# How the last four blocks of an output projection join its sum in a decode attention kernel

## The chip, the core and the metric

The kernel runs on one core of one Trainium2 chip. TensorE (PE) multiplies, VectorE (DVE) and ScalarE (ACT) work on vectors, GpSimd (POOL) only fills constants here, and SyncE (SP) issues transfers. The metric is the device time of one execution in microseconds (us); for several runs the median is given.

## The reference

One decode step for two sequences (batch 2, one token, width 512). A layer norm of `x` feeds two branches. The first is attention of 32 query heads on 8 key/value heads, over the last 4096 positions of a cache, and a projection by `wo` (4096 x 512). The second is a small gated network, whose result gates the first:

```python
x = A_x
xn = _layernorm(x, axis=-1)
s = _A_ref(xn, A_k_cache, A_v_cache, A_wq, A_wo)     # softmax(q k / sqrt(128)) v, then @ wo
g = _silu(_B_ref(xn, B_w_in, B_w_sp, B_b_sp, B_w_out))
return x + s * g
```

All is f32. Keys and values of the window are 64 MB of the 89.4 MB that the kernel reads; `wo` is 8 MB.

## The kernel before, in words

Every large transfer is issued by SP into a ring of four slots of 4 MB: `w_in`, `w_out`, two halves of `wq`, then keys and values in turn for eight units (a unit is two key/value heads of one sequence), then `wo`. The gated branch and the queries are computed first. For each unit, DVE transposes the keys (`turn`), PE multiplies them in shares (`shares`, `add_shares`), DVE and ACT make the softmax, and PE multiplies the values (`values`, `scale_out`, `collect`). The transposed outputs of all heads end in `oT`, 32 columns for each of 32 blocks, of which two columns hold the two sequences.

`wo` comes in 32 blocks of 128 rows by 512 columns (256 KB). They arrive in seven transfers (line 423): 8 and 8 blocks in one slot, 8 in a second, and 4, 2, 1, 1 in a third. So blocks 24 to 27 come together, then 28 and 29, then 30, then 31, each transfer with a semaphore of its own that PE waits for ahead of the first matmul that reads it.

The tail (lines 480 to 500) adds `oT` times the blocks in two ways.

- *By shares*: block n is one matmul of 512 columns into rows 32g to 32g+31 of the PSUM bank `part`, with g = n mod 4. So each of the four groups of 32 rows holds the sum of a fourth of the blocks, over all 512 columns. ACT copies the bank to `parts` in SBUF, and `spread_quarters` (line 250) adds the four shares: for each quarter of the columns, one matmul with the constant `rowm` sums the four groups into rows 32g to 32g+31 of a second bank `so`.
- *By column quarters*: block n is four matmuls of 128 columns, each straight into its quarter of `so`. That is four instructions in place of one, and no copy stands between them and the result.

Before the change, blocks 0 to 29 go by shares (`EARLY = 30`). Then come the copy, the spread, which opens the accumulation in `so`, and blocks 30 and 31 by quarters, which close it. DVE multiplies `so` by the gate, adds `x`, and SP and ACT each store one sequence.

The order on each engine is the order of the program text (`InOrder` keeps it), so on PE an instruction that waits holds up all that follow. Since that helper records every operation, all rows of the profile have its line, L37; they are told apart by the names of their tiles.

Of the kernel before, what the change touches and what calls it, by code (L numbers as in the profile page):

```python
# [42 lines left out]
def kernel(  # L43
# [23 lines left out]
    DC = D // G  # L67
# [13 lines left out]
    def slot(name):  # L81
        return ring.tile([P, SLOT], F32, tag="slot", name=name)

    def const(name, *shape):
        return cst.tile([P, *shape], F32, tag=name, name=name)

    def bank(name, tag):
        return ps.tile([P, 512], F32, tag=tag, name=name, bufs=BANKS[tag])
# [12 lines left out]
    for a in range(2):  # L101
        t = slot(f"wq{a}")
# [37 lines left out]
    oT = const("oT", 32, 32)  # L140
# [61 lines left out]
    for k in range(KT):  # L202
        for g in range(G):
            pe.matmul(
                pz[32 * g : 32 * g + 32, :], xnT[:, k, :], ap(win[:, k, :], g * FQ, [[FH, 2], [1, FQ]]),
                start=(k == 0), stop=(k == KT - 1),
# [43 lines left out]
    def spread_quarters(dst, shares, start=True, stop=True):  # L250
        for g in range(G):
            pe.matmul(
                dst[32 * g : 32 * g + 32, :], rowm, shares[:, g * DC : (g + 1) * DC], start=start, stop=stop,
            )

    yp = bank("y", "sh")
    for j in range(FT):
        g = j % G
# [14 lines left out]
    for k in range(KT):  # L273
        for r in range(2):
            for g in range(G):
# [3 lines left out]
                    start=(k == 0), stop=(k == KT - 1),  # L279
# [145 lines left out]
    for i, piece in enumerate(pieces):  # L425
        t = slot(f"wo{i}").rearrange("p (j d) -> p j d", d=D)
# [50 lines left out]
    gather(last)  # L477


    EARLY = 30  # L480
    part = bank("part", "sh")
    for n in range(EARLY):
        t, a = blocks[n]
        g = n % G
        pe.matmul(part[32 * g : 32 * g + 32, :], oT[:, n, :], t[:, a, :], start=(n < G), stop=(n >= EARLY - G))
    parts = sb.tile([P, D], F32, tag="shs", name="parts")
    act.activation(parts, part, AF.Copy)
    so = bank("so", "mo")[:, :DC]
    spread_quarters(so, parts, stop=False)
    for n in range(EARLY, 32):  # L490
        t, a = blocks[n]
        for g in range(G):
            pe.matmul(
                so[32 * g : 32 * g + 32, :], oT[:, n, :], t[:, a, g * DC : (g + 1) * DC], start=False, stop=(n == 31),
            )
    res = const("res", DC)
    dve.tensor_mul(res, so, gate)
# [31 lines left out]
```

## Time and profile before

| what | value |
|---|---|
| median of 3 runs | 219.26 us (218.83 to 219.28) |
| profiled execution | 219.14 us |
| its span, first to last instruction | 217.4 us |
| mean granted TensorE clock | 0.851 |
| PE busy | 156.1 us (72%) |
| DVE busy | 108.6 us (50%) |
| ACT busy | 44.0 us (20%) |
| read from HBM | 89.40 MB, 411 GB/s over the span |

Times in the profile count from the start of the span. A row of the timeline has the start, the length, the engine, the operation, the tiles (out<-in), the shape and the count of a group of equal instructions; in brackets stands how long the engine was idle before and what ended that. PEld rows are weight loads of TensorE, PE rows its matmuls. The chain of waits goes back from the last instruction through whatever released each step.

### The profile page before, as it was taken

What the parts mean: (1) busy time and instruction counts of PE and PEld (TensorE: products, weight loads), DVE (VectorE), ACT (ScalarE), POOL (GpSimd) and SP (SyncE); (2) the same over time, 40 slices, a digit from 0 to 9 for tenths busy, and PEclk for the clock granted to TensorE, in tenths of its full rate; (3) what the DMA queues carried; (4) which work ended last, traced back from release to release, by engine and by line L of the source; (5) the groups of instructions that cost most, each with busy time, mean ns of one, the idle gap of its engine ahead of it and who ended that gap; (6) DMA issues with size and microseconds to landing.
All of it is one profiled execution on the core that took longest, in us unless ns stands there. A gap on an engine that the chain in (4) does not pass through costs nothing.

```text
span 217.4 us, 2207 instructions
## 1 busy us (share of the span) xinstructions
PE 156.1 (72%) x854; PEld 43.4 (20%) x854; DVE 108.6 (50%) x176; ACT 44.0 (20%) x109; POOL 2.6 (1%) x14
## 2 busy tenths in 40 slices
PE   0173185519959948975996797469959949997991
PEld 0121121101212212211221221322221212232211
DVE  3505411579787089148707932594577189221001
ACT  5003310002221421122114212120430421142001
POOL 4000000000000000000000000000000000000000
PEclk9997579955988995998599799757996996999599
DMA  7999999999999999999999999999999999999970
GB/s 254 430 444 446 416 442 419 446 416 452 416 452 410 443 422 446 416 452 416 436 425 428 434 428 419 446 416 452 410 440 425 440 422 440 410 425 423 416 296 4
DMA packets 3937, 89.54 MB, mean 412 GB/s; under 512 B 454, under 2 KB 470, under 8 KB 856
## 3 DMA queue, kind: packets, MB, share of 16 engines
q1 hardware_dynamic: 3912, 89.40, 96.2%
q8 instruction: 7, 0.11, 0.2%
q10 hardware_dynamic: 16, 0.01, 0.0%
q14 instruction: 2, 0.02, 0.0%
HBM read 89.40 MB, written 0.00 MB: 411 GB/s over the span
## 4 chain that ended last, share of the span: by engine, by line
DMA 62%; DVE 19%; PE 16%; issue 1%; ACT 0%; DVEq 0%; SPq 0%; ACTq 0%
DMA k<-in_A_k_cache_dram 49%; DVE kt L37 15%; DMA wo<-in_A_wo_dram 8%; DMA win<-in_B_w_in_dram 5%; PE sh L37 5%; PE s L37 4%; PE z L37 2%; PE acc L37 2%; PE mo L37 1%; DVE pT L37 1%; DVE m L37 1%; PE part L37 0%; PE oT L37 0%; PE so L37 0%; DVE mg L37 0%
## 5 line engine op out<-in xcount | busy, mean ns | idle before, releaser
L37 DVE STREAM_TRANSPOSE kt<-k 128x2048 f32<-128x2048 f32 x32 | 72.7, 2295 | 41.7 <-DMA k<-in_A_k_cache_dram 41.7
L37 PE MATMUL sh<-kt,qbd 128*32 128x512 f32 x256 | 41.0, 704 | 17.4 <-DVE kt L37 17.4
L37 ACT ACTIVATE shs<-sh 128x512 f32<-128x512 f32 x32 | 19.1, 597 | 119.4 <-PE sh L37 119.4
L37 PE MATMUL s<-shs,add_dq 128*128 128x512 f32 x64 | 40.4, 738 | 0.0
L37 PE MATMUL acc<-v,pT 128*32 128x512 f32 x256 | 33.0, 659 | 0.2 <-DVE pT L37 0.2
L37 PEld LDWEIGHTS s<-shs,add_dq 128*128 128x128 f32 x64 | 11.1, 216 | 29.8 <-issue 25.4
L37 PEld LDWEIGHTS sh<-kt,qbd 128*32 128x32 f32 x256 | 6.4, 114 | 37.9 <-issue 23.4
L37 PEld LDWEIGHTS acc<-v,pT 128*32 128x32 f32 x256 | 7.8, 121 | 26.9 <-issue 19.3
L37 PE MATMUL mo<-l,same_r 128*128 128x2 f32 x16 | 3.5, 287 | 10.6 <-ACT p L37 10.6
L37 PE MATMUL part<-wo,oT 128*32 128x512 f32 x60 | 10.4, 808 | 0.6 <-issue 0.4
L37 ACT ACTIVATE o<-acc,wd 128x128 f32<-128x128 f32 x32 | 9.1, 372 | 3.4 <-PE acc L37 3.4
L37 ACT ACTIVATE p<-s,nb 128x256 f32<-128x256 f32 x16 | 7.6, 490 | 7.2 <-DVE nb L37 6.9
L37 PE MATMUL q_ps<-wq,xnT 128*32 128x512 f32 x64 | 7.3, 594 | 2.4 <-DMA wq<-in_A_wq_dram 2.4
L37 PE MATMUL z<-win,xnT 128*32 128x448 f32 x32 | 5.2, 818 | 4.8 <-DMA win<-in_B_w_in_dram 4.8
L37 PE MATMUL col<-o,sel 128*32 128x512 f32 x16 | 8.3, 601 | 0.4 <-ACT o L37 0.4
L37 DVE TENSOR_REDUCE m<-s 128x2 f32<-128x512 f32 x8 | 5.4, 670 | 4.9 <-PE s L37 4.9
L37 DVE TENSOR_TENSOR res<-so,gate 128x128 f32<-128x128 f32 x1 | 0.3, 291 | 12.4 <-PE so L37 12.4
L37 PE MATMUL y<-wout,hT 128*32 128x512 f32 x14 | 3.2, 975 | 3.8 <-issue 3.8
L37 DVE STREAM_TRANSPOSE pT<-p 128x512 f32<-128x512 f32 x8 | 5.4, 674 | 1.2 <-ACT p L37 1.2
L37 ACT ACT_TABLE_LOAD x4 | 5.1, 1283 | 2.0 <-issue 1.9
L37 PE MATMUL xnT_ps<-ident,xn 2*128 2x2 f32 x4 | 0.6, 253 | 6.6 <-DVE xn L37 6.6
L37 PEld LDWEIGHTS mo<-l,same_r 128*128 128x128 f32 x16 | 2.8, 218 | 12.2 <-ACT p L37 12.2
(106 smaller groups left out, 63.1 us busy)
## 6 DMA issues: line engine op xcount, KB each, us to landing
k<-in_A_k_cache_dram SPq DMA_DIRECT2D x8, 4096.0 KB, 26.4
v<-in_A_v_cache_dram SPq DMA_DIRECT2D x8, 4096.0 KB, 32.2
wq<-in_A_wq_dram SPq DMA_DIRECT2D x2, 4096.0 KB, 29.6
wo<-in_A_wo_dram SPq DMA_DIRECT2D x3, 2048.0 KB, 28.2
win<-in_B_w_in_dram SPq DMA_DIRECT2D x1, 3584.0 KB
wout<-in_B_w_out_dram SPq DMA_DIRECT2D x1, 1792.0 KB, 15.0
wo<-in_A_wo_dram SPq DMA_DIRECT2D x1, 1024.0 KB, 17.1
wo<-in_A_wo_dram SPq DMA_DIRECT2D x1, 512.0 KB, 17.9
```

What stands on the lines that cost most here:

```text
L37: return self.tc.keep_in_program_order(call(*args, **kwargs))
```

## The change

Blocks 0 to 27 go by shares (`EARLY = 28`). Blocks 28 and 29 go by column quarters into `so` and now stand between the copy of `part` and the spread; block 28 opens the accumulation in each quarter. Then comes the spread, which adds to it, and blocks 30 and 31 follow by quarters as before. Transfers, their order and all other work stay as they are.

```diff
-    EARLY = 30
+    EARLY, LATE = 28, 30
     part = bank("part", "sh")
     for n in range(EARLY):
         t, a = blocks[n]
...
     parts = sb.tile([P, D], F32, tag="shs", name="parts")
     act.activation(parts, part, AF.Copy)
     so = bank("so", "mo")[:, :DC]
-    spread_quarters(so, parts, stop=False)
     for n in range(EARLY, 32):
+        if n == LATE:
+            spread_quarters(so, parts, start=False, stop=False)
         t, a = blocks[n]
         for g in range(G):
             pe.matmul(
-                so[32 * g : 32 * g + 32, :], oT[:, n, :], t[:, a, g * DC : (g + 1) * DC], start=False, stop=(n == 31),
+                so[32 * g : 32 * g + 32, :], oT[:, n, :], t[:, a, g * DC : (g + 1) * DC],
+                start=(n == EARLY), stop=(n == 31),
             )
```

## The prediction

> **What bounds the kernel now.** I read the page first (span, chain), then the chain of waits, then the timeline of the last eight microseconds, then each of the last four transfers alone.
>
> ```profile
> span 217.4 us, 2207 instructions
> ...
> DMA 62%; DVE 19%; PE 16%; issue 1%; ACT 0%; DVEq 0%; SPq 0%; ACTq 0%
> ```
>
> The profiled execution took 219.14 us: the span and 1.7 us around it. Most of the chain is transfers, so compute that lies beside them is worth nothing. The change touches only what follows the attention units. There the chain of waits of the kernel before reads (start, us, what):
>
> ```profile
> 192.93 17.94 DMA wo<-in_A_wo_dram
> 210.86 0.04 issue
> 210.91 1.08 PE part L37 x4
> ...
> 212.07 0.60 ACT parts L37
> 212.67 0.04 issue
> 212.72 0.91 PE so L37 x24
> 213.62 0.02 issue
> 213.65 0.30 DVE res L37
> ```
>
> The transfer issued at 192.93 is the third-last piece of `wo` (blocks 28 and 29). It lands at 192.93 + 17.94 = 210.87. From there everything is in series: two blocks into `part`, the copy, the spread with blocks 30 and 31, the gate. `res` starts 213.65 - 210.87 = 2.78 us behind that landing. The timeline shows the same stretch by rows:
>
> ```profile
> 209.66 0.16 PEld L37 LDWEIGHTS part<-wo,oT 128*32 128x32 f32 x8 [0.96 <-DMA wo<-in_A_wo_dram]
> 210.90 0.14 PEld L37 LDWEIGHTS part<-wo,oT 128*32 128x32 f32 x4 [1.09 <-DMA wo<-in_A_wo_dram]
> 210.91 1.05 PE L37 MATMUL part<-wo,oT 128*32 128x512 f32 x4 [0.18 <-DMA wo<-in_A_wo_dram]
> 212.07 0.60 ACT L37 ACTIVATE parts<-part 128x512 f32<-128x512 f32 x1 [14.24 <-PE part L37]
> 212.72 0.42 PE L37 MATMUL so<-parts,rowm 128*32 128x128 f32 x8 [0.76 <-ACT parts L37]
> 212.85 0.46 PEld L37 LDWEIGHTS so<-wo,oT 128*32 128x32 f32 x16
> 212.96 0.62 PE L37 MATMUL so<-wo,oT 128*32 128x128 f32 x16
> 213.65 0.29 DVE L37 TENSOR_TENSOR res<-so,gate 128x128 f32<-128x128 f32 x1 [12.40 <-PE so L37]
> ```
>
> Each f32 matmul of the program stands as two load rows and two matmul rows. So the x8 at 209.66 are blocks 24 to 27, and the x4 at 210.90 are blocks 28 and 29. PE idles twice for a landing there, then once for the copy (0.76 us). The next rows come from narrow windows, which cut a group apart: the last four rows of blocks 24 to 27, the first four of the spread, the last four of block 31.
>
> ```profile
> 210.11 0.61 PE L37 MATMUL part<-wo,oT 128*32 128x512 f32 x4
> ...
> 212.72 0.32 PE L37 MATMUL so<-parts,rowm 128*32 128x128 f32 x4 [0.76 <-ACT parts L37]
> ...
> 213.28 0.29 PE L37 MATMUL so<-wo,oT 128*32 128x128 f32 x4
> ```
>
> Blocks up to 27 are summed by 210.11 + 0.61 = 210.72, before block 28 has landed. The 24 rows of `so` run from 212.72 to 212.96 + 0.62 = 213.58, which is 0.86 us.
>
> The landings decide the rest. Each of the last four issues alone, with its time to landing (blocks 24 to 27; 28 and 29; 30; 31):
>
> ```profile
> 192.55 0.33 SPq L37 DMA_DIRECT2D wo<-in_A_wo_dram  x1
> DMA to landing us min/median/max: 17.1/17.1/17.1
> ...
> 192.93 0.43 SPq L37 DMA_DIRECT2D wo<-in_A_wo_dram  x1
> DMA to landing us min/median/max: 17.9/17.9/17.9
> ...
> 193.41 0.42 SPq L37 DMA_DIRECT2D wo<-in_A_wo_dram  x1
> DMA to landing us min/median/max: 18.1/18.1/18.1
> ...
> 197.34 0.33 SPq L37 DMA_DIRECT2D wo<-in_A_wo_dram  x1
> DMA to landing us min/median/max: 14.8/14.8/14.8
> ```
>
> They land at 209.65, 210.87 (by the chain), 211.51 and 212.14. Block 31 is there 0.58 us before the spread starts now, so its landing is hidden; it will not be hidden after the change.
>
> **The change, part by part.**
>
> *Out of `part`.* Two matmuls of 512 columns leave (four load and four matmul rows, 1.05 us behind the landing). The copy's last input becomes block 27, complete at 210.72. From the last `part` row to the copy it takes 212.07 - (210.91 + 1.05) = 0.11 now; so the copy runs from 210.83 to 211.43 with its 0.60. Now it ends at 212.67, so it is 1.24 us earlier. That is the gain if nothing else comes in.
>
> *Into `so`, under the copy.* Blocks 28 and 29 return as eight matmuls of 128 columns (16 loads, 16 matmul rows), six matmuls more than before. They wait for the landing at 210.87 and start at 210.91, as block 28 does now. They go four rows at a time, one for each quarter. From rest, the first two fours of `so` and the start of the third lie 212.96 - 212.72 = 0.24 us apart, and each later four starts (213.28 - 212.96) / 3 = 0.11 after the one ahead. So PE could begin the spread at 210.91 + 0.24 + 2 x 0.11 = 211.37, and the quarters' last row ends at 210.91 + 0.32 + 3 x 0.11 = 211.56. The copy releases the spread only at 211.43 + 0.05 = 211.48 (212.72 behind 212.67 now). I cost this part at nothing: its cover is PE's wait for the copy, with 0.11 us to spare. What runs over that pushes the spread, which then has 0.24 us more before it counts, by the step after next.
>
> *The moved wait.* The wait for blocks 28 and 29 stood ahead of the last `part` matmuls and now stands ahead of the first `so` matmul. Behind it on PE are only the spread and the last two blocks; ACT no longer depends on it. No DMA, and no queue of SP or POOL, is touched. Matmuls on PE during a copy don't slow the copy, as far as the rows tell:
>
> ```profile
> L37 ACT ACTIVATE shs<-sh 128x512 f32<-128x512 f32 x32 | 19.1, 597 | 119.4 <-PE sh L37 119.4
> ```
>
> Those 32 copies, of the same shape, ran amid busy PE at a mean of 597 ns; the one of `parts`, with PE idle, took 0.60.
>
> *What is late next.* The spread starts at 211.48. Its eight rows let block 30 start at 211.48 + 0.24 = 211.72; block 30 landed at 211.51, so no wait. Block 31 could start at 211.72 + 2 x 0.11 = 211.94, but lands at 212.14. Its load starts 0.04 later, 212.18 (the issue gap of the chain), and PE has idled by then, so its eight rows take 0.42: done at 212.60. Today the end is 213.58. Both are followed by the same gate, sum and output. The gain is 213.58 - 212.60 = 0.98 us: 1.24 from the copy less 0.26 for block 31.
>
> The landing of block 31 is the one term that the kernel before doesn't show as a wait. Bounds by the rows: if it came by 211.9, nothing would wait and `so` would end at 211.48 + 0.86 = 212.34 (gain 1.24). On the late side, the last three landings trail each other by 0.64 and 0.63; one such step more would put it at 212.77 and leave a gain of 0.35. I take 212.14, the row itself, since nothing that issues or feeds that transfer changes.
>
> The sum: 219.14 - 0.98 = 218.16 us against the profiled execution's own time. That stands 0.12 under the median of 219.26, and from the median it would be 218.28; I say 218.2.
>
> **The rivals.**
>
> *No wait at the end* (block 31 there early, or the four landings closer together): 219.14 - 1.24 = 217.9. For it speaks that traffic dies down before 212; against it, the 14.8.
>
> ```profile
> 211.25:211.50 0.25, 0.25 (x4) 0.00 (x0) 0.00 (x0) 0.00 (x0) 0.00 (x0) 1.00 0.13 49
> 211.50:212.00 0.50, 0.46 (x4) 0.00 (x0) 0.00 (x0) 0.00 (x0) 0.00 (x0) 1.00 0.19 41
> 212.00:213.00 1.00, 0.28 (x12) 0.29 (x16) 0.00 (x0) 0.60 (x1) 0.00 (x0) 1.00 0.00 0
> ```
>
> The last two columns are the DMA share and GB/s: data still moved after 211.50, so 211.9 is not far off. The clock before them is 1.00 throughout, so no rate above shifts.
>
> *A later landing*: the end follows the last of 16 DMA engines directly, where 0.58 us of slack covered it. At 212.77 the time is 218.8.
>
> *The copy still waits for the quarters* (the change doesn't do what it says): the quarters end at 211.56, the copy would run from 211.67 to 212.27, and `so` would end at 212.32 + 0.86 = 213.18: gain 0.40, 218.7. Against it: the copy reads `part` alone, and its last writer is now block 27.
>
> *An instruction fetch comes ahead of the last data* (the slower side). The next rows are the DMA view of the stretch from 211.8 to 213.4 in slices of 0.04 us:
>
> ```profile
> DMA  0009000000000000000000000000000000000000
> ...
> q8 instruction: 1, 0.02, 5.2%
> ```
>
> One packet of 0.02 MB starts at about 211.93, and 5.2% of 16 engines over 1.6 us is 1.33 us of one engine. If six more matmuls drew it before the last piece on the engine that ends last, block 31 would land at 213.47 and `so` end at 213.93, 0.35 later than now: 219.5. It decides from 0.98 us of delay on. Against it: PE's rows up to block 27 are unchanged, and the packet now follows them by 1.2 us, while data ends before 212. The Trainium skill (Runtime: NRT & Kernel Launch, Instruction fetch mechanics) has such fetches as blocks of 256 instructions taken in order and mostly hidden; by that, 24 rows more would move none, and the trace's single packet in this stretch agrees.
>
> *Loads that don't overlap.* If the loads of the quarters could not run under matmuls of the other quarters, each of the ten groups of four behind 210.91 (load row 0.11, matmul row 0.27 from the next lines) would take 0.38: the end would come at 214.71, 1.13 later than now, and the time at 220.3.
>
> ```profile
> L37 PEld LDWEIGHTS so<-wo,oT x16: 110/110/111, 212.8 to 213.2; 128*32 128x32 f32 x16
> L37 PE MATMUL so<-wo,oT x16: 272/273/273, 213.0 to 213.3; 128*32 128x128 f32 x16
> ```
>
> Against it: by the same count the six groups of now would take 2.28 us, and they took 0.86. The Trainium skill (TensorE: Matmul & The Clock Gate, Part 3: Packing small matmuls, The mechanism) says that a weight load overlaps running matmuls only where the row group differs; all rows here use the same 128 rows, so by that rule the change would lose. The trace disagrees: 16 loads from 212.85 on lie inside the matmuls' 212.72 to 213.58.
>
> **How the numbers follow.** Forecast 0.68; no wait 0.10; later landing 0.10; copy waits 0.05; fetch 0.05; serial loads 0.02. 218.2 is the first case. The range goes from 218.83 - 1.24 = 217.6 (the fastest run before, no wait) to 218.9 (the slowest run, 219.28, less 0.35): it leaves out the fetch and the serial loads and a bit of noise. What a measurement here can tell from no change is 0.2%, 0.44 us. Faster: forecast, no wait and most of the later landings, 0.86. Same: the other landings, the waiting copy, half of the fetch, 0.10. Slower: the rest, 0.04.
>
> **What would show it.** Right: the copy of `parts` starts about 210.83, with PE rows of `so<-wo` during it; the spread at about 211.48; then eight last rows whose load waited for a DMA of `wo`, at about 212.18; `res` at about 212.67. Wrong: a copy that starts behind 211.6 (the third rival), last rows without a wait (the first), a landing of the last piece after 212.6 (the second), a q8 packet before 211.7 (the fourth), or quarters spread over more than a microsecond (the fifth).

## The result, and the profile after

The changed kernel takes 218.17 us (median of 6 runs, 217.97 to 218.33) against 219.13 (6 runs, 218.83 to 219.28) for the kernel before: ratio 0.9957, 95% interval 0.9944 to 0.9970. The profiled execution took 217.97 us, with a span of 216.3.

Absolute times of two executions differ by some tenths already where the tail begins, since the transfers don't land at the same moment. So the tails below are compared from a landing on. The chain of waits of the changed kernel (start, us, what):

```profile
197.20 14.82 DMA wo<-in_A_wo_dram
212.02 0.04 issue
212.06 0.47 PE so L37 x8
212.53 0.02 issue
212.56 0.30 DVE res L37
```

Before, this chain came from the landing of blocks 28 and 29, through `part` and the copy. Now it comes from the transfer issued at 197.20, the very last piece (block 31). It lands at 197.20 + 14.82 = 212.02, and eight matmul rows and the gate are all that follow: `res` starts 212.56 - 212.02 = 0.54 us behind it. The copy and the spread have left the chain.

The timeline of the same stretch:

```profile
209.52 0.16 PEld L37 LDWEIGHTS part<-wo,oT 128*32 128x32 f32 x8 [1.47 <-DMA wo<-in_A_wo_dram]
209.52 1.07 PE L37 MATMUL part<-wo,oT 128*32 128x512 f32 x8 [0.56 <-DMA wo<-in_A_wo_dram]
210.72 0.60 ACT L37 ACTIVATE parts<-part 128x512 f32<-128x512 f32 x1 [12.66 <-PE part L37]
210.79 0.38 PEld L37 LDWEIGHTS so<-wo,oT 128*32 128x32 f32 x16 [1.11 <-DMA wo<-in_A_wo_dram]
210.79 0.65 PE L37 MATMUL so<-wo,oT 128*32 128x128 f32 x16 [0.20 <-DMA wo<-in_A_wo_dram]
211.36 0.16 PEld L37 LDWEIGHTS so<-parts,rowm 128*32 128x32 f32 x8 [0.20 <-ACT parts L37]
211.37 0.42 PE L37 MATMUL so<-parts,rowm 128*32 128x128 f32 x8
...
211.61 0.88 PE L37 MATMUL so<-wo,oT 128*32 128x128 f32 x16
212.06 0.16 PEld L37 LDWEIGHTS so<-wo,oT 128*32 128x32 f32 x8 [0.32 <-DMA wo<-in_A_wo_dram]
212.56 0.29 DVE L37 TENSOR_TENSOR res<-so,gate 128x128 f32<-128x128 f32 x1 [11.31 <-PE so L37]
```

The 16 rows of blocks 28 and 29 lie under the copy (210.72 to 211.32) and end 0.12 us behind it, at 211.44, when the spread is already running. The loads ahead of the spread waited for the copy (0.20 us of idle), so the quarters did not delay it. Then the loads of block 31 waited 0.32 us for a DMA of `wo`. That row did not exist before. Of the x16 at 211.61, the first eight are block 30 and the last eight block 31.

From the landing of blocks 28 and 29 to `res` it was 213.65 - 210.87 = 2.78 us. It is now 212.56 - 210.75 = 1.81 (the landing being 0.04 ahead of 210.79). The difference, 0.97 us, agrees with the medians' 219.13 - 218.17 = 0.96.

### The profile page after: what moved, and what is told of

Its sections match the earlier page's. It is cut to its first block, busy times and chain, and to the rows that moved or that the text cites. A ratio compares the mean times of both kernels' runs of the same rounds, so it can differ in the third digit from the quotient of the medians.

```text
span 216.3 us, 2231 instructions
## 1 busy us (share of the span) xinstructions
PE 153.6 (71%) x866; PEld 43.2 (20%) x866; DVE 108.5 (50%) x176; ACT 44.0 (20%) x109; POOL 2.6 (1%) x14
## 4 chain that ended last, share of the span: by engine, by line
DMA 63%; PE 19%; DVE 15%; issue 1%; DVEq 0%
DMA k<-in_A_k_cache_dram 38%; DMA wo<-in_A_wo_dram 21%; DVE kt L37 12%; PE sh L37 6%; DMA win<-in_B_w_in_dram 5%; PE s L37 5%; PE acc L37 3%; PE z L37 3%; PE mo L37 1%; DVE m L37 1%; DVE pT L37 1%; PE oT L37 0%; PE col L37 0%; DVE mg L37 0%; DVE mx L37 0%
## 5 line engine op out<-in xcount | busy, mean ns | idle before, releaser
L37 PE MATMUL sh<-kt,qbd 128*32 128x512 f32 x256 | 41.7, 727 | 20.2 <-DVE kt L37 20.2
L37 PE MATMUL acc<-v,pT 128*32 128x512 f32 x256 | 30.6, 618 | 0.2 <-DVE pT L37 0.2
L37 PE MATMUL part<-wo,oT 128*32 128x512 f32 x56 | 8.1, 712 | 1.5 <-DMA wo<-in_A_wo_dram 1.1
```

The lines of the kernel that those rows point to most:

```text
L37: return self.tc.keep_in_program_order(call(*args, **kwargs))
```

## The experiments

The theory: before, the copy's wait for blocks 28 and 29 set the end; now the landing of block 31 plus 0.54 us sets it, and what is freed beyond that is lost in the wait for it. The rivals are that the work moved under the copy makes the gain, that the chain through copy and spread still sets the end, or that the end simply follows the bytes. Each ratio is to runs of the kernel before from the same session; their median was 219.35 us in one session and 219.25 in the other, against 219.13 above, so ratios and not times are compared from one experiment to the next.

**One part undone: nothing under the copy.**

```diff
-    EARLY, LATE = 28, 30
+    EARLY, LATE = 28, 28
...
-            spread_quarters(so, parts, start=False, stop=False)
+            spread_quarters(so, parts, start=True, stop=False)
...
-                start=(n == EARLY), stop=(n == 31),
+                start=False, stop=(n == 31),
```

> One part undone: blocks 28 to 31 all go by quarters behind the spread, so nothing is multiplied under the copy; the copy still needs blocks 0 to 27 alone. Theory (the copy's earlier start makes the gain, the last landing limits it): the spread starts about 211.4 as in the changed kernel, then 16 + 16 more rows in series; so ends about 212.67 instead of 212.49, behind the last landing without waiting for it. res about 0.18 us later than in the changed kernel: 218.35 us, ratio to before about 0.9965. Rival (the gain is the work moved under the copy): without that work under the copy nothing is left, 219.1, ratio 1.000.

Measured: ratio 0.9963, interval 0.9950 to 0.9976 (218.55 us). Most of the gain stays, so it isn't the moved work as such; it is that the copy waits for less. The chain of waits of this kernel:

```profile
193.53 16.21 DMA wo<-in_A_wo_dram
209.74 0.04 issue
209.78 1.11 PE part L37 x8
...
210.98 0.60 ACT parts L37
211.58 0.04 issue
211.63 1.34 PE so L37 x40
212.97 0.02 issue
212.99 0.30 DVE res L37
```

It starts at the landing of blocks 24 to 27 (209.74), the copy's new last input, and all 40 rows of `so` stand in series behind the copy. From that landing to `res` it is 212.99 - 209.74 = 3.25 us. In the changed kernel it is 212.56 - 209.48 = 3.08 (the landing 0.04 ahead of 209.52). So putting 16 rows under the copy is worth 0.17 us net by the profiles. In series the 16 rows cost more, 0.43 us (1.34 for 40 rows here, 0.91 for 24 in the kernel before); but this kernel no longer waits for the landing of block 31, and that gives back the 0.26 that the changed kernel loses there. The times (0.9963 against 0.9957) have the same order, but their intervals overlap.

**One more transfer ahead of block 31, in the changed kernel and in the kernel before.**

```diff
         for n in piece:
+            if j == 31:
+                sp.dma_start(t[:, at + 2 : at + 3, :], wo_v[:, 0:1, :])
             sp.dma_start(t[:, at : at + n, :], wo_v[:, j : j + n, :])
```

> The changed kernel with one more transfer of 256 KB (block 0 of wo again, into an unused part of the slot, read by nobody) between the transfers of blocks 30 and 31. Theory (the end is the landing of block 31 plus a fixed 0.54 us to res): block 31 lands about 0.63 us later (the step between the last landings before), and the end moves by all of it: about 218.8, ratio to before about 0.9985. Rival (the chain through copy and spread binds, the landing is at most a short wait): the end moves by less than 0.3 us, 218.2 to 218.5.

> The kernel before with the same extra transfer of 256 KB between blocks 30 and 31. Theory: block 31 lands at about 212.8 and is first needed at about 213.18 (spread 212.72, block 30, block 31), so the landing stays hidden: no change, 219.1 to 219.2, ratio 0.999 to 1.001. Rival (more bytes cost their time wherever they are): 0.6 us slower, ratio 1.003.

Measured: 0.9985 (0.9975 to 0.9994) in the changed kernel and 1.0004 (0.9992 to 1.0016) in the kernel before. The same 256 KB cost the changed kernel 0.28% of 219, 0.61 us, and the other nothing that can be measured (by its interval at most 0.35 us, where that rival has 0.6). Changed kernel with the transfer, chain and loads:

```profile
202.43 10.57 DMA wo<-in_A_wo_dram
213.00 0.04 issue
213.05 0.47 PE so L37 x8
...
213.54 0.30 DVE res L37
...
211.14 0.65 PE L37 MATMUL so<-wo,oT 128*32 128x128 f32 x16 [0.21 <-DMA wo<-in_A_wo_dram]
...
213.04 0.16 PEld L37 LDWEIGHTS so<-wo,oT 128*32 128x32 f32 x8 [0.96 <-DMA wo<-in_A_wo_dram]
```

Block 31 landed 213.00 - 211.10 = 1.90 us behind blocks 28 and 29 (the landing being 0.04 ahead of 211.14), where it was 212.02 - 210.75 = 1.27 without the transfer: 0.63 later, as one more landing step was taken for. The wait grew by the same, from 0.32 to 0.96 us. `res` stands 0.54 us behind the landing, as without the transfer. The kernel before with the same transfer, chain:

```profile
211.06 1.08 PE part L37 x4
...
212.22 0.60 ACT parts L37
212.82 0.04 issue
212.87 0.91 PE so L37 x24
...
213.80 0.30 DVE res L37
```

Its chain is that of the kernel before, step by step, with 0.91 us from spread to end, so no wait came in. By the last count on its semaphore in the trace, block 31 landed at 212.92, behind the start of the spread, and its loads followed at 213.22 without idle time. The end became sensitive to the last landing through the change.

**The transfer of block 31 left out, in both kernels.**

```diff
-    pieces = ((8, 8), (8,), (4, 2, 1, 1))
+    pieces = ((8, 8), (8,), (4, 2, 1))
...
+    blocks.append(blocks[-1])
```

> The changed kernel without the transfer of block 31: its matmuls use block 30's weights instead, so the last product is another one; all instructions of PE stay. Theory: no landing is waited for behind the spread; so ends about 0.26 us earlier (spread 211.37, 0.86 us of rows, end 212.23 instead of 212.49): 217.9, ratio to before about 0.9945. Rival (the chain binds, no landing counts): 218.2, ratio 0.9957. Second rival (bytes bind, the end follows the last landing wherever it is): 0.63 us earlier, 217.5.

> The kernel before without the transfer of block 31: its matmuls use block 30's weights instead, so the last product is another one; all instructions of PE stay. Theory: that landing was hidden by about a microsecond before the change, and res stands 2.78 us behind the landing of blocks 28 and 29 as before; nothing in the tail moves: 218.9 to 219.3, ratio 0.998 to 1.001 (a little below 1 if fewer bytes bring the other landings forward). Rival (the end follows the last bytes wherever they are): 0.6 us earlier, ratio 0.997.

Measured: 0.9933 (0.9917 to 0.9948) and 0.9995 (0.9985 to 1.0005). So without that landing the changed kernel gains again, and the kernel before doesn't. The further gain in the changed kernel rests on the chain more than on the times, whose interval still touches that with all transfers (0.9944 to 0.9970). In the first, the time alone doesn't part the theory (0.9945) from the second rival (217.5, 0.993); the chain does:

```profile
193.25 17.38 DMA wo<-in_A_wo_dram
210.64 0.04 issue
210.68 1.49 PE so L37 x40
212.17 0.02 issue
212.19 0.30 DVE res L37
```

All 40 rows of `so` run in one piece (with the copy's wait inside) from the landing of blocks 28 and 29, now at 193.25 + 17.38 = 210.63. `res` follows that landing by 1.56 us, against 1.81 in the changed kernel: 0.25 us less, where 0.26 was expected for the wait. What the median has beyond that came with earlier landings in this kernel, or is scatter; the runs don't tell. The kernel before, without the transfer:

```profile
210.92 0.04 issue
210.96 1.08 PE part L37 x4
...
213.70 0.30 DVE res L37
```

`res` is 213.70 - 210.92 = 2.78 us behind the landing of blocks 28 and 29, as with all transfers.

**A still earlier copy.**

```diff
-    EARLY, LATE = 28, 30
+    EARLY, LATE = 24, 30
```

> Four more blocks are taken out of the shares: blocks 24 to 29 go by quarters ahead of the spread, so the copy needs blocks 0 to 23 alone and starts about 1.6 us earlier than in the changed kernel. Theory: the copy no longer limits anything, the landing of block 31 does; so ends where it does in the changed kernel: 218.2, ratio to before about 0.9957, and PE's wait for the landing of block 31 grows by about 0.1 us. Rival (the copy's start still sets the end): up to 1.2 us faster than the changed kernel, 217.0, ratio 0.990.

Measured: 0.9952 (0.9940 to 0.9965), 218.17 us. Nothing is gained over the changed kernel that can be told apart. Timeline of this kernel:

```profile
209.91 0.60 ACT L37 ACTIVATE parts<-part 128x512 f32<-128x512 f32 x1 [10.47 <-PE part L37]
210.03 0.81 PEld L37 LDWEIGHTS so<-wo,oT 128*32 128x32 f32 x32 [1.15 <-DMA wo<-in_A_wo_dram]
...
211.26 0.38 PEld L37 LDWEIGHTS so<-wo,oT 128*32 128x32 f32 x16 [0.41 <-DMA wo<-in_A_wo_dram]
...
212.53 0.16 PEld L37 LDWEIGHTS so<-wo,oT 128*32 128x32 f32 x8 [0.46 <-DMA wo<-in_A_wo_dram]
...
213.02 0.29 DVE L37 TENSOR_TENSOR res<-so,gate 128x128 f32<-128x128 f32 x1 [10.38 <-PE so L37]
```

The copy starts 0.12 us ahead of the first loads of blocks 24 to 27, where the changed kernel has it 1.20 behind (209.52 to 210.72). So it came 1.3 us earlier, not the 1.6 that I had expected. All of it is lost, most of it already ahead of the spread: blocks 28 and 29 stand there, and their loads now wait 0.41 us for their own landing, so the spread's matmuls start at 211.72, 0.50 us behind that landing, where it was 0.62 in the changed kernel. The rest is lost at block 31, whose wait grew from 0.32 to 0.46; and `res` is 0.49 us behind the start of block 31's loads, as 212.56 is behind 212.06 to within 0.01.

**The spread behind block 31, and block 30 ahead of the spread.**

The first of two edits to the order on PE:

```diff
-    EARLY, LATE = 28, 30
+    EARLY = 28
...
-        if n == LATE:
-            spread_quarters(so, parts, start=False, stop=False)
...
-                start=(n == EARLY), stop=(n == 31),
+                start=(n == EARLY), stop=False,
             )
+    spread_quarters(so, parts, start=False, stop=True)
```

> The spread moved behind block 31, so that blocks 28 to 31 go by quarters in the order of their landings and the spread closes the sum. Theory: behind the landing of block 31 now stand 16 rows in place of 8, 0.22 us more: 218.4, ratio about 0.9967; before that landing PE waits longer (about 0.45 us). Rival (order on PE doesn't matter, since its rows overlap): 218.2, ratio 0.9957.

And the second:

```diff
-    EARLY, LATE = 28, 30
+    EARLY, LATE = 28, 31
```

> Block 30 moved ahead of the spread (three blocks ahead of it, one behind). Theory: block 30 lands about 0.03 us after the copy ends, so the spread starts about 0.2 to 0.3 us later, but its rows end before the landing of block 31; behind that landing stand the same 8 rows: no change against the changed kernel, 218.2, ratio about 0.9957. Rival (each delay of the spread delays the end): 0.25 us slower than the changed kernel, ratio 0.9968.

Measured: 0.9960 (0.9947 to 0.9973) and 0.9956 (0.9942 to 0.9969). The times can't tell 0.1% apart; the profiles can. The chain with the spread last:

```profile
197.33 14.80 DMA wo<-in_A_wo_dram
212.14 0.04 issue
212.18 0.69 PE so L37 x16
212.87 0.02 issue
212.89 0.30 DVE res L37
```

Sixteen rows behind the last landing take 0.69 us where eight take 0.47: the 0.22 that was expected. The timeline with block 30 ahead of the spread (quarters, block 30, spread, block 31):

```profile
211.02 0.38 PEld L37 LDWEIGHTS so<-wo,oT 128*32 128x32 f32 x16 [1.10 <-DMA wo<-in_A_wo_dram]
...
211.68 0.16 PEld L37 LDWEIGHTS so<-wo,oT 128*32 128x32 f32 x8 [0.28 <-DMA wo<-in_A_wo_dram]
211.82 0.24 PEld L37 LDWEIGHTS so<-parts,rowm 128*32 128x32 f32 x8
211.93 0.40 PE L37 MATMUL so<-parts,rowm 128*32 128x128 f32 x8
212.31 0.16 PEld L37 LDWEIGHTS so<-wo,oT 128*32 128x32 f32 x8 [0.25 <-DMA wo<-in_A_wo_dram]
...
212.80 0.29 DVE L37 TENSOR_TENSOR res<-so,gate 128x128 f32<-128x128 f32 x1 [10.98 <-PE so L37]
```

The spread's loads start 0.80 us behind those of blocks 28 and 29 (211.82 - 211.02); in the changed kernel it is 0.57 (211.36 - 210.79). The spread is 0.23 us later, and `res` still stands 0.49 behind the start of block 31's loads. The delay fell into the room before the last landing and nearly filled it: the spread's matmuls end at 211.93 + 0.40 = 212.33, with block 31's following at once. So the chain view of this kernel runs through PE without naming that landing; that it was still waited for shows in the 0.25 us that the loads of block 31 stood idle for a DMA of `wo`, with the spread's loads done at 211.82 + 0.24 = 212.06.

No order tried here beats the changed kernel: at least eight rows and the gate stand behind the last landing in all of them.

## Why the prediction was right

The forecast was 218.2 us with a gain of 0.98; measured were 218.17 and 0.96. That the times agree to 0.03 us is luck, since runs of the changed kernel lie up to 0.36 us apart. The two terms agree without it. Counted from the landing of blocks 28 and 29, the spread started 1.85 us behind it before (212.72 - 210.87) and 0.62 now (211.37 - 210.75), 1.23 earlier where the copy was to bring 1.24. The last row of `so` ended 2.71 behind it before (213.58 - 210.87) and 1.74 now (212.49 - 210.75), 0.97 earlier; so 0.26 is lost at block 31, as forecast.

- *Out of `part`.* The copy was to start 1.17 us behind the first loads of blocks 24 to 27 (210.83 less 209.66). It started 1.20 behind (210.72 less 209.52), with the same 0.60 of its own. The third rival (the copy still waits for the quarters) is out: the copy started at 210.72, before the quarters did at 210.79.
- *Into `so`, under the copy.* 16 rows were taken at 0.65 us (210.91 to 211.56) and took 0.65. That they cost nothing holds: the loads of the spread waited for the copy. With that part undone they stood in series behind the copy and cost 0.17 us by the profiles, the price of the lost cover.
- *What is late next.* Block 31's loads were to start 0.04 us behind its landing and its rows to take 0.42; they started at 212.06 behind 212.02 and took 0.43 (the 0.88 from 211.61 end at 212.49). The landing held as forecast because its distance held: 1.27 us behind blocks 28 and 29 in both kernels (212.14 - 210.87, 212.02 - 210.75). The first rival (no wait) and the second (a later landing) were the two ends of this term. The transfer left out gave the one, 0.25 us faster from landing to `res`, and the transfer added gave the other, 0.61 slower. Two readings in the prediction were off here, without effect on the sum. The slack that covered this landing before was not the 0.58 us to the spread, which doesn't read block 31, but about 0.9 us, to the block's own loads (0.35 us behind the spread's start with the added transfer, 213.22 less 212.87). And most of what was read as data after 211.50 (41 GB/s for 0.50 us is 0.02 MB) is the fetched packet of 0.02 MB, so it says little about when block 31 lands.
- *The fetch.* The next rows are the DMA view of the changed kernel from 211.7 to 213.3:

```profile
DMA  0009000000000000000000000000000000000000
...
q8 instruction: 1, 0.02, 4.3%
```

The packet starts at about 211.83, with block 27 summed at 209.52 + 1.07 = 210.59. It stood 1.2 us behind that sum before and stands 1.2 behind now. It did not come ahead of the last data: no packet starts between 211.6 and 211.8. Six matmuls more drew no further packet: the page of the profile counts seven on that queue in both kernels. That they would draw none did not follow from the rows of before, which don't show where one fetched block ends and the next begins; the count settles it.

- *Loads that don't overlap.* The 16 loads of blocks 28 and 29 took 0.38 us from 210.79 and lie inside the 0.65 of their matmuls. The fifth rival is out by the changed kernel's own row as well. The rule of the Trainium skill that was weighed there (TensorE: Matmul & The Clock Gate, Part 3: Packing small matmuls, The mechanism), that a load overlaps running matmuls only where the row group differs, doesn't hold for these matmuls, which share all rows and differ by column group. The same section names one more way, a load into a background weight buffer; the runs don't tell whether that is what these loads do.

## What to carry to other kernels

Where a reduction is fed by transfers that land one after the other, ask of each later stage (here a copy) which landing its last input waits for, and let only what has landed by then go through it; the rest can take a way with more instructions, best where the engine was waiting anyway (here that place was worth 0.17 us of 0.97). Such a change pays until the end hangs on the last landing alone. From there, only what stands behind that landing counts, and an earlier copy or another order ahead of it buys nothing. Whether the end hangs on a landing is told by a small extra transfer ahead of it: 256 KB cost 0.61 us where it did and nothing where it did not.

## What the runs showed that I had not expected

The landings move from one execution to the next by more than most of the differences studied here. Blocks 28 and 29 landed at 210.63 in one profiled execution (the last transfer left out) and at 211.22 in another (the copy after block 23), though their transfers are the same. The last landings move together: block 31 came 1.22 to 1.29 us behind blocks 28 and 29 in the kernel before, the changed one, the still earlier copy and both edits to the order. And distances from a landing repeat. From the last landing to `res` it was 0.53 or 0.54 us in the four kernels that wait for it with eight rows to come: the changed one, the one with a transfer more, the still earlier copy (213.02 less 212.53, plus the 0.04 between landing and loads), and block 30 ahead of the spread. From the landing of blocks 28 and 29 to `res` it was 2.78 or 2.79 in the three profiles of the old order. So differences of 0.1 to 0.25 us could be read from one profile each, taken from landing to end, where five timed runs left an interval of 0.25%.
